# Top-k attention into a mixture of experts: the mask of every third later tile is added by GpSimd

## The chip, the cores and the metric

One core of one Trainium2 chip. The time is that of one execution on the device in microseconds (us); smaller is better. Engine names in the profile: PE is TensorE's matmuls, PEld its weight loads, DVE is VectorE, ACT ScalarE, POOL GpSimd, SP the queue that issues most transfers.

## The reference

Attention over 8 batches of 8 heads, 576 positions, 64 values per head, in which each row keeps its 32 largest scores; then a mixture of 8 experts in which each of the 4608 rows goes to one expert.

```python
scores = scale * np.matmul(q, k.transpose(0, 1, 3, 2))
kth = np.partition(scores, -top_k, axis=-1)[..., -top_k:-top_k + 1]
scores = np.where(scores >= kth, scores, -1000000000.0)
scores = scores - np.max(scores, axis=-1, keepdims=True)
attn = np.exp(scores)
attn = attn / (np.sum(attn, axis=-1, keepdims=True) + 1e-09)
attn_out = np.matmul(attn, v)
...
h = np.maximum(x[mask] @ w1[e], 0.0)
out[mask] = gate_w[mask, None] * (h @ w2[e])
```

## The kernel before

The attention is cut into 288 tiles of 128 rows by 576 scores (9 tiles for each pair of heads, 36 for a batch). One written-out loop of 310 iterations is a software pipeline over them: iteration i computes the scores of tile i+2 on TensorE (`qk`, L336), copies them to SBUF on ScalarE (`sevac`, L342, ten buffers), takes the maxima of seven pieces of tile i on VectorE (`subs`, L349), merges those of tile i-1 to its 24 largest (`chain`, L360 to L362), and lets GpSimd note a bound for them (`below`, L374). Three iterations later ScalarE marks which scores lie below the bound (`sign`, L381), GpSimd multiplies mark and scores (`pool_y`, L387), and VectorE finds the next eight (`find`, L391). Every third iteration `pick` (L398 to L400) sets the 32nd largest, `kth`, for three tiles at once.

The probabilities of tile u = i-7 come at the end of VectorE's share of iteration i. There are two ways. In the first, ScalarE has taken the exponential of all scores an iteration earlier (`expo`, L405), and VectorE compares with `kth`, multiplies and sums in one instruction (`keep`, L411). GpSimd then runs a one-element instruction on the result (`gate`, L434) ahead of its next product L387. In the second, VectorE writes 0 or a large negative number as bfloat16 (`hide`, L418), GpSimd adds it to the scores at the start of its share of iteration u+8 (`hidden`, L424), and ScalarE takes the exponential of the sum and its row sums (`masked`, L430). Which way a tile goes is said by `early(u)`. In the kernel before it is true for two of three tiles up to the 48th, whose masks lie in `hT`, a buffer that the experts need later.

After that TensorE transposes the probabilities (`trans`, L445), ScalarE copies them (`evac`, L453), and `av` multiplies with the values (L473). When a batch is through, its rows are scaled, routed and sent to their expert's place in DRAM: five indirect transfers (`send`, L564), issued by GpSimd, one to an iteration for the second batch on; they stand among VectorE's small steps, ahead of `gate` and `pool_y` in GpSimd's order and behind `hidden`. From then on the loop also carries pieces of the experts' matmuls (L727, L739), as many to an iteration as a written-out budget of TensorE time allows; their output transfers (L754) stand at the end of GpSimd's iteration. Behind the loop, from some 1062 us on, the rest of the experts follows in three-term products.

Each engine runs its own instructions in the order of the program. On GpSimd an iteration's order is: `hidden`, sends and other small steps, `gate`, `pool_y`, `below`, `small` (L368), `fill` (L314), output transfers. On ScalarE: `sign`, copies of the experts' results, `expo`, `sevac`, `evac`, `masked`, splits of the next heads.

`zr` is a constant tile of zeros, which pads the experts' lists in DRAM; its last pad is issued in iteration 26.

Of the kernel before, what the change touches and what calls it, by code (L numbers as in the profile page):

```python
# [11 lines left out]
BF = mybir.dt.bfloat16  # L12
# [51 lines left out]
EARLY = 48  # L64
# [7 lines left out]
def kernel(  # L72
# [14 lines left out]
    B, H, S, D = q.shape  # L87
# [104 lines left out]
    hT = const.tile([128, FC, SLOT], FT, name="hT")  # L192
# [16 lines left out]
    zr = const.tile([128, XW], FT, name="zr")  # L209
# [203 lines left out]
    def hide(i):  # L413

        t = T[i]
        x = 2 * (i % 2)
        t["hb"] = hT[:, x:x + 2, :].rearrange("p f t -> p (f t)").bitcast(BF)[:, :S]
        V.tensor_scalar(t["hb"], t["S"], kth[:, i:i + 1], -HUGE, op0=OP.is_lt, op1=OP.mult)  # L418

    def hidden(i):  # L420
# [34 lines left out]
    def av(p, j, x):  # L455

        vm, vt = LD[p]["v"]
        w = 256 if j < 8 else 64
        st = {}

        def part(c0, c1):
            if c0 == 0:
                st["po"] = psX.tile([128, 256], FT, name="X")
            po = st["po"]
            for c in range(c0, c1):
                for h in range(2):
                    l = vm[:, h, c, :] if c < 4 else vt[:, h if j < 8 else 2 * h, :]
                    if j < 8:
                        r = PT[:, j // 2 - 1:j // 2 + 1, c + 5 * h if c < 4 else 4, :]
                    else:  # L470
                        r = PT[:, 1, 4 + c, h * 64:h * 64 + 64]
                    o = po[h * 64:h * 64 + 64, :w]
                    PE.matmul(o.rearrange("p (a b) -> p a b", a=2) if j < 8 else o, l, r, start=(c == 0), stop=(c == 4))  # L473
            if c1 == 5:
                o = (j // 4) * 256
                xev.append(lambda: A.activation(x[:, o:o + w], po[:, :w], AF.Copy))
        cut = {3: AV3, 7: AV7, 8: (0, 5)}[j]
        return [((b - a) * COST["av" if j < 8 else "av8"], lambda a=a, b=b: part(a, b)) for a, b in zip(cut, cut[1:])]
# [398 lines left out]
        qk(x, 0, x, qbd[0])  # L877
        sevac(x)
    ok = lambda x: 0 <= x < NT
    early = lambda u: u < EARLY and u % 3 != 2  # L880
    dn_of = lambda u: den[(u // 36) % 2][:, (u // 9) % HP, u % 9:u % 9 + 1]
    PREP = dict(zip(PJ, "tkq"))
    spare_pe = 0.0
# [3 lines left out]
    for i in range(LAST):  # L887
# [8 lines left out]
        p, j = divmod(i, 9)  # L896
        u = i - TL
# [11 lines left out]
        u = i - (KL + 1)  # L909
# [6 lines left out]
        u = i - LE  # L916
# [6 lines left out]
        u = i - TL  # L923
        if ok(u):
            evac(u)
        u = i - LR - 1
# [46 lines left out]
        u = i - (TL + 1)  # L973
        if avs:
            c, f = avs.popleft()
            f()
            cost += c
        if ok(u) and u % 9 in (3, 7, 8):
            f = av(u // 9, u % 9, xTs(u // 36)[(u // 9) % HP])
# [9 lines left out]
        while seen[0] and spare_pe > 0:  # L989
# [4 lines left out]
            c, f, new = moe[0]  # L994
# [25 lines left out]
        for x in range(RN if rush else 0):  # L1020
            f = rush.popleft() if rush else PAUSE
# [6 lines left out]
        for x in range(SN - len(small_)):  # L1028
            f = side.popleft() if side and not rush else PAUSE
# [6 lines left out]
        if ok(i - LR):  # L1036
            u = i - LR
            c_.append(lambda u=u: hide(u) if early(u) else keep(u, dn_of(u)))
# [284 lines left out]
```

## Time and profile before

| what | value |
|---|---|
| median of 3 runs | 1294.74 us (1290.1 to 1295.56) |
| profiled execution | 1286.85 us, its span 1285.1 us |
| PE, PEld busy | 1183.2 us (92%), 934.1 us (73%) |
| DVE busy | 1157.5 us (90%) |
| ACT busy | 996.6 us (78%) |
| POOL busy | 665.8 us (52%) |
| granted TensorE clock, mean | 0.984 |

The share of an engine is a mean over stages: the loop over the tiles fills some 20 to 1062 us, the experts' rest the last 220 us. What a change in the loop is worth is read from the loop alone. A busy engine can still be one that waits: TensorE's ends are modelled, and each instruction's end lies beside the start of the next one. So starts are compared with starts.

### The profile page before, as it was taken

How to read it: one execution, taken by the hardware profiler on the slowest of the kernel's cores; microseconds unless marked ns; L12 is line 12 of the kernel's file. 1: busy time of each engine (PE TensorE's matmuls, PEld its weight loads, DVE VectorE, ACT ScalarE, POOL GpSimd, SP SyncE). 2: the span in 40 equal slices, each digit the busy share in tenths (PEclk: the TensorE clock that was granted, in tenths of full speed). 3: DMA queues.
4: the chain of work that ended last, by engine and by line, in shares of the span. 5: the costliest groups of instructions: out<-in, count | busy, mean ns of one | idle time of the engine just before them, and what ended most of it. 6: DMA issues, size and time to landing. Idle time of an engine off the chain costs nothing. (4 is left out here: it accounts for less than half of the span.)

```text
span 1285.1 us, 29038 instructions
## 1 busy us (share of the span) xinstructions
PE 1183.2 (92%) x8117; PEld 934.1 (73%) x8117; DVE 1157.5 (90%) x5948; ACT 996.6 (78%) x2029; POOL 665.8 (52%) x1249
## 2 busy tenths in 40 slices
PE   5789887999988999999999999999999999999996
PEld 4667676767766778686777868777777766789885
DVE  4999999999999999999999999999999992767752
ACT  3799988888888988888898889888988773446542
POOL 2688866555474557554755575556655562110110
PEclk8899999999999999999999999999999999999998
DMA  6565336765347745755665665656766433657550
GB/s 125 125 183 142 89 85 183 198 156 149 85 128 189 216 124 154 199 158 127 194 169 159 168 187 147 171 143 171 170 154 168 132 122 115 234 186 266 204 171 15
DMA packets 206755, 201.05 MB, mean 156 GB/s; under 512 B 106221, under 2 KB 153325, under 8 KB 206576
## 3 DMA queue, kind: packets, MB, share of 16 engines
q1 hardware_dynamic: 198896, 178.59, 52.6%
q0 software_dynamic: 6256, 19.69, 4.2%
q8 instruction: 69, 1.13, 0.4%
q10 hardware_dynamic: 1424, 0.74, 0.2%
q14 instruction: 110, 0.90, 0.2%
HBM read 118.63 MB, written 24.23 MB: 111 GB/s over the span
## 5 line engine op out<-in xcount | busy, mean ns | idle before, releaser
L349 DVE MAX8 cand<-Ssb 128x8 f32<-128x82 f32 (+1 forms) x2016 | 429.4, 230 | 17.9 <-ACT Ssb L342 17.7
L387 POOL TENSOR_TENSOR y<-Ssb,K 128x576 f32<-128x576 f32 x288 | 367.8, 1277 | 1.9 <-ACT K L381 1.6
L336 PE MATMUL S<-ks,qs 128*128 128x288 f32 x1024 | 230.1, 347 | 43.1 <-ACT Ssb L342 24.5
L342 ACT ACTIVATE Ssb<-S 128x576 f32<-128x576 f32 x288 | 188.7, 655 | 91.4 <-PE S L336 61.7
L381 ACT ACTIVATE K<-Ssb,n 128x576 bf16<-128x576 f32 x288 | 227.5, 790 | 25.3 <-POOL y L387 25.1
L336 PEld LDWEIGHTS S<-ks,qs 128*128 128x128 f32 x1024 | 157.4, 192 | 97.0 <-issue 40.5
L391 DVE MAX8 mg<-y 128x8 f32<-128x576 f32 x288 | 214.4, 745 | 2.7 <-POOL y L387 2.7
L405 ACT ACTIVATE ex<-Ssb,sm 128x576 f32<-128x576 f32 x256 | 200.3, 782 | 0.0
L453 ACT ACTIVATE PT<-T 128x640 f32<-128x640 f32 (+1 forms) x288 | 191.1, 663 | 9.5 <-PE T L445 9.5
L727 PE MATMUL E<-xgT,w1b 128*128 128x256 f32 x768 | 187.6, 387 | 6.8 <-ACT hT L731 3.1
L411 DVE SCALAR_TENSOR_TENSOR P<-Ssb,kth,ex 128x576 f32<-128x576 f32 x224 | 188.6, 842 | 0.3
L739 PE MATMUL E<-w2b,hT 128*128 128x512 f32 x384 | 179.6, 596 | 3.0 <-ACT ot L749 1.7
L445 PE MATMUL T<-idf,P 128*128 128x128 f32 x1152 | 171.9, 277 | 9.5 <-ACT P L430 8.9
L727 PEld LDWEIGHTS E<-xgT,w1b 128*128 128x128 f32 x768 | 139.8, 192 | 31.6 <-ACT hT L731 6.4
L434 POOL TENSOR_SCALAR spare<-P 1x1 f32<-1x1 f32 x224 | 43.6, 195 | 201.7 <-DVE mg L360 186.8
L445 PEld LDWEIGHTS T<-idf,P 128*128 128x128 f32 x1152 | 136.0, 141 | 16.7 <-ACT P L430 13.3
L473 PE MATMUL X<-PT,vm 128*64 128x256 f32 (+1 forms) x1536 | 145.6, 332 | 2.4 <-DVE cand L349 1.1
L374 POOL TENSOR_SCALAR n<-mg 128x1 f32<-128x1 f32 x288 | 72.8, 253 | 133.6 <-DVE mg L362 127.0
L473 PEld LDWEIGHTS X<-PT,vm 128*64 128x64 f32 x1536 | 89.2, 137 | 47.8 <-issue 10.1
L739 PEld LDWEIGHTS E<-w2b,hT 128*128 128x128 f32 x384 | 67.2, 190 | 60.6 <-issue 53.2
L1166 POOL DMA_INDIRECT out_dram<-ot,tk x14 | 14.0, 1003 | 132.3 <-ACT ot L1165 132.3
L862 PE MATMUL E<-idf,onesb 128*128 128x256 bf16 x436 | 63.1, 285 | 0.0
(212 smaller groups left out, 2295.8 us busy)
## 6 DMA issues: line engine op xcount, KB each, us to landing
w1b<-in_moe_w_dram SPq DMA_DIRECT2D x76, 512.0 KB, 5.0
w2b<-in_moe_w_dram SPq DMA_DIRECT2D x76, 512.0 KB, 4.9
qs<-st SPq DMA_DIRECT2D x126, 144.0 KB, 3.5
ks<-st SPq DMA_DIRECT2D x63, 288.0 KB, 3.8
ks<-st SPq DMA_DIRECT2D x62, 256.0 KB, 5.2
xg<-xs SPq DMA_DIRECT2D x19, 516.0 KB, 3.9
km<-in_k_dram SPq DMA_DIRECT2D x64, 128.0 KB, 3.5
vm<-in_v_dram SPq DMA_DIRECT2D x32, 256.0 KB, 3.2
```

The source lines that it names most:

```text
L336: PE.matmul(ps[:, hf, u - a:v - a], l, d["ks"][:, x, h, u + o:v + o], start=(n == 0), stop=(n == len(terms) - 1), skip_group_check=(j == 8))
L342: A.activation(sb.rearrange("p (a b) -> p a b", a=2), T[i]["ps"][:, :, :288], AF.Copy, scale=0.125)
L349: return [lambda s=s: V.max(c[:, s * 8:s * 8 + 8], T[i]["S"][:, bnd[s]:bnd[s + 1]]) for s in range(NSUB)]
L381: A.activation(t["K"], t["S"], AF.Sign, scale=2.0 ** -24 - 1.0, bias=t["n"][:, 1, i % 3:i % 3 + 1], accum_out=t["n"][:, 0, i % 3:i % 3 + 1])
L387: G.tensor_tensor(t["y"], t["S"], t["K"], op=OP.mult)
L391: V.max(t["mg"][:, i % 3, 24:32], t["y"])
L405: A.activation(t["ex"], t["S"], AF.Exp, bias=t["s"][:, i % 3:i % 3 + 1])
L445: PE.transpose(T[i]["pt"][:, x, :], (Pm if c == 4 else Pb[c % 2])[:, h * 512 + x * 128:h * 512 + x * 128 + 128], idf)
L453: A.activation(o, T[i]["pt"][:, :n], AF.Copy)
L473: PE.matmul(o.rearrange("p (a b) -> p a b", a=2) if j < 8 else o, l, r, start=(c == 0), stop=(c == 4))
L727: PE.matmul(ps[:, f % 2], w1b[:, c, f * 128:(f + 1) * 128], xgT[:, c, :], start=(c == 0), stop=(c == KC - 1))
L739: PE.matmul(o["py"], hT[:, f, t * 128:(t + 1) * 128], w2b[:, f, :], start=(f == 0), stop=(f == FC - 1))
```

## The change

From tile 48 on, every tile whose number divides by three goes the second way: `hide`, `hidden` and `masked` take the place of `expo`, `keep` and `gate` for it. These are 80 tiles. Their mask lies in `zr` in place of `hT`. The two other tiles of three stay as they are, and so do the first 48.

```diff
-        t["hb"] = hT[:, x:x + 2, :].rearrange("p f t -> p (f t)").bitcast(BF)[:, :S]
+        t["hb"] = (hT[:, x:x + 2, :].rearrange("p f t -> p (f t)") if i < EARLY else zr).bitcast(BF)[:, :S]
         V.tensor_scalar(t["hb"], t["S"], kth[:, i:i + 1], -HUGE, op0=OP.is_lt, op1=OP.mult)
...
-    early = lambda u: u < EARLY and u % 3 != 2
+    early = lambda u: u % 3 != 2 if u < EARLY else u % 3 == 0
```

## Rows read from the trace of the kernel before

**Rows 1.** The page's second part: busy tenths of TensorE and VectorE in 40 equal slices of the span (32 us each).

```profile
PE   5789887999988999999999999999999999999996
DVE  4999999999999999999999999999999992767752
```

**Rows 2.** Busy time of each engine by window: early tiles, and the stretch that the change touches. Columns: length, PE, PEld, DVE, ACT, POOL (instructions), granted clock, DMA share, GB/s.

```profile
48.00:198.00 150.00, 129.59 (x1090) 103.50 (x1091) 150.00 (x825) 136.06 (x308) 119.34 (x167) 0.99 0.48 119
198.00:1062.00 864.00, 821.90 (x5601) 632.80 (x5600) 851.93 (x4621) 739.36 (x1519) 501.43 (x976) 0.99 0.61 161
```

**Rows 3.** VectorE's costliest groups from 198 to 1062 us: count | busy us, mean ns | idle us before them, and who ended it.

```profile
L349 DVE MAX8 cand<-Ssb 128x8 f32<-128x82 f32 x1161 | 260.7, 231 | 0.0
L411 DVE SCALAR_TENSOR_TENSOR P<-Ssb,kth,ex 128x576 f32<-128x576 f32 x213 | 178.4, 838 | 0.3
L391 DVE MAX8 mg<-y 128x8 f32<-128x576 f32 x237 | 176.8, 746 | 2.7 <-POOL y L387 2.7
```

**Rows 4.** Who waited for whom from 198 to 1062 us: us in total, times, longest.

```profile
ACT Ssb L342 <- PE S L336: 39.7, 46, 2.3
ACT K L381 <- POOL y L387: 25.1, 47, 1.7
...
PE S L336 <- ACT Ssb L342: 19.3, 25, 2.3
```

**Rows 5.** VectorE in order of time, a tile that divides by three and the next one: start us, us, what.

```profile
943.31 0.82 DVE L411 SCALAR_TENSOR_TENSOR P<-Ssb,kth,ex 128x576 f32<-128x576 f32 x1
944.06 0.08 DVE L411 DVE_READ_ACCUMULATOR P<-Ssb,kth,ex 128x1 f32 x1
...
946.48 0.80 DVE L411 SCALAR_TENSOR_TENSOR P<-Ssb,kth,ex 128x576 f32<-128x576 f32 x1
```

**Rows 6.** VectorE in order of time among the early tiles: two instructions L418, what follows each, and the L411 behind the second.

```profile
116.54 0.49 DVE L418 TENSOR_SCALAR hT<-Ssb,kth 128x576 bf16<-128x576 f32 x1
116.95 0.20 DVE L360 MAX8 mg<-cand 128x8 f32<-128x56 f32 x1
...
119.37 0.58 DVE L418 TENSOR_SCALAR hT<-Ssb,kth 128x576 bf16<-128x576 f32 x1
119.87 0.20 DVE L360 MAX8 mg<-cand 128x8 f32<-128x56 f32 x1
...
122.29 0.96 DVE L411 SCALAR_TENSOR_TENSOR Pm<-Ssb,kth,ex 128x576 f32<-128x576 f32 x1
123.18 0.08 DVE L411 DVE_READ_ACCUMULATOR Pm<-Ssb,kth,ex 128x1 f32 x1
```

**Rows 7.** GpSimd in order of time beside the second half of rows 6.

```profile
118.36 1.28 POOL L387 TENSOR_TENSOR y<-Ssb,K 128x576 f32<-128x576 f32 x1
...
120.10 1.28 POOL L424 TENSOR_TENSOR ex<-Ssb,hT 128x576 f32<-128x576 f32 x1
121.34 1.29 POOL L387 TENSOR_TENSOR y<-Ssb,K 128x576 f32<-128x576 f32 x1
```

**Rows 8.** GpSimd in order of time beside rows 5 (in brackets: idle before it, and who ended that).

```profile
944.30 0.18 POOL L434 TENSOR_SCALAR spare<-P 1x1 f32<-1x1 f32 x1 [1.43 <-DVE mg L360]
944.45 1.27 POOL L387 TENSOR_TENSOR y<-Ssb,K 128x576 f32<-128x576 f32 x1
```

**Rows 9.** VectorE in order of time: end of a step L411 and start of the next L411, for the first (tile 60) and the last (tile 279) of the 32 tiles that divide by three, have a gap of at most 2.50 us and no send in their iteration.

```profile
244.03 0.08 DVE L411 DVE_READ_ACCUMULATOR P<-Ssb,kth,ex 128x1 f32 x1
...
246.44 0.80 DVE L411 SCALAR_TENSOR_TENSOR P<-Ssb,kth,ex 128x576 f32<-128x576 f32 x1
...
1042.33 0.08 DVE L411 DVE_READ_ACCUMULATOR P<-Ssb,kth,ex 128x1 f32 x1
...
1044.74 0.80 DVE L411 SCALAR_TENSOR_TENSOR P<-Ssb,kth,ex 128x576 f32<-128x576 f32 x1
```

**Rows 10.** GpSimd's groups from 198 to 1062 us: the sends.

```profile
L564 POOL DMA_INDIRECT xs<-x,dest x35 | 37.5, 1073 | 7.9 <-issue 4.2 <-DVE cand L349 2.5 <-DVE mg L360 0.8
```

**Rows 11.** VectorE in order of time within one burst of sends: two instructions L411 and the end of their steps.

```profile
757.72 1.93 DVE L411 SCALAR_TENSOR_TENSOR P<-Ssb,kth,ex 128x576 f32<-128x576 f32 x1
759.58 0.08 DVE L411 DVE_READ_ACCUMULATOR P<-Ssb,kth,ex 128x1 f32 x1
...
761.99 1.38 DVE L411 SCALAR_TENSOR_TENSOR P<-Ssb,kth,ex 128x576 f32<-128x576 f32 x1
763.31 0.08 DVE L411 DVE_READ_ACCUMULATOR P<-Ssb,kth,ex 128x1 f32 x1
```

**Rows 12.** GpSimd in order of time beside rows 11.

```profile
757.76 1.27 POOL L387 TENSOR_TENSOR y<-Ssb,K 128x576 f32<-128x576 f32 x1
...
760.12 1.03 POOL L564 DMA_INDIRECT xs<-x,dest  x1 [0.16 <-issue]
...
761.48 1.27 POOL L387 TENSOR_TENSOR y<-Ssb,K 128x576 f32<-128x576 f32 x1
```

**Rows 13.** Line 411 over the whole span: shortest/median/longest ns, first and last start us.

```profile
L411 DVE SCALAR_TENSOR_TENSOR P<-Ssb,kth,ex x224: 787/802/1930, 47.6 to 1059.2; 128x576 f32<-128x576 f32 x112
```

**Rows 14.** Groups of the whole span: the exponential of the first way, the add and the exponential of the second.

```profile
L405 ACT ACTIVATE ex<-Ssb,sm 128x576 f32<-128x576 f32 x256 | 200.3, 782 | 0.0
...
L424 POOL TENSOR_TENSOR ex<-Ssb,hT 128x576 f32<-128x576 f32 x32 | 41.1, 1284 | 17.6 <-DVE hT L418 10.9 <-DVE mg L360 5.5
...
L430 ACT ACTIVATE P<-ex,sm 128x576 f32<-128x576 f32 x32 | 25.2, 788 | 0.0
```

## The prediction

> **What bounds the kernel now.** I read the busy digits first, then the stretch that the change touches, then who waits there, then single instructions. The change starts with tile 48; that tile's probability step stands near 198 us and the last one ends near 1062 us. In that stretch VectorE is busy for 851.9 of 864 us; TensorE shows 821.9, ScalarE 739.4, GpSimd 501.4 [rows 1, 2]. Two engines near full, so the question is which one waits for the other. VectorE's sub-maxima L349, the first thing it does with new scores, had 0.0 us of idle time ahead of 1161 of them, and the full-row maximum L391 2.7 us in 237 tiles [rows 3]: VectorE's inputs are ready before it wants them. TensorE does wait, for the copy that frees its scores buffer (19.3 us), ScalarE waits for scores (39.7 us) and for GpSimd's product (25.1 us) [rows 4]. So VectorE sets the pace, and what is taken off it in this stretch should come off the time, as long as the others' slack holds. TensorE's granted clock is 0.99 and is no part of this.
>
> A busy time overstates VectorE's cost, since one instruction's end overlaps the next one's start. I count steps instead: from an instruction's start to the start of the next on the engine.
>
> **The change part by part.** From tile 48 on, 80 tiles (48, 51, ... 285) go the hidden way.
>
> *VectorE, removed and added.* L411 is a step of 0.75 us (943.31 to 944.06) [rows 5]. L418 in its place was 0.41 us (116.54 to 116.95) where no GpSimd product ran beside it, and 0.50 where 0.27 us of one did [rows 6, 7]. In the new order the third-tile's L418 comes late in an iteration, when GpSimd's product is long done (the product ends at 945.72, the next L411 starts at 946.48 [rows 5, 8]), so I take 0.42. Saved: 80 x 0.33 = 26 us, all of it on the pacing engine.
>
> *What the next tile pays for it.* Today GpSimd runs gate and product L387 behind L411: both are over 1.66 us after L411's step ends (944.06 to 945.72) [rows 5, 8]. Behind L418 it runs the add L424 and then L387, over 2.76 us after (119.87 to 122.63) [rows 6, 7]. The next tile's L411 can start 2.42 us after (122.29; the same 2.42 from 944.06 to 946.48) [rows 5, 6]. So the tail of L387 runs into it by 0.34 us, and L411 took 0.89 us there in place of 0.75 [rows 6]: 0.14 given back. Where VectorE has other small work in that iteration, L411 starts later and escapes. I took the gap from the end of L411's step to the next L411 for the 78 tiles 48 to 279: 38 are at most 2.50 us (the first of the plain ones and the last are in [rows 9]), 13 lie between 2.50 and 2.75, 27 are longer. Six of the 38 belong to the bursts below. 32 x 0.14 + 13 x 0.07 = 5.4 us given back.
>
> The row says that 0.34 us of overlap cost 0.14. The Trainium skill, "SBUF — State Buffer", section "Who interferes with whom", says that a VectorE instruction with two SBUF inputs contends with a GpSimd instruction that reads SBUF, and that the pair of ports is an exclusive lock for a whole instruction; by that the cost would be the 0.34 whole, 32 x 0.34 + 13 x 0.15 = 13 us in place of 5.4.
>
> *The bursts of sends.* Each batch from the second on sends its rows in five GpSimd transfers L564, one to an iteration, of 1.07 us each; the window has 35, of which 30 are of this kind [rows 10]. They are queued ahead of gate today, so they run beside L411 and cost it nothing. The add is queued ahead of them: L424, then L564, then L387, which then begins about 2.8 us after L418 and sits on the next L411 from its start. What that costs the trace shows in one burst: an L411 that began with L387 took 1.86 us (757.72 to 759.58), one with 0.76 us of L387 left took 1.32 [rows 11, 12]: 1.1 and 0.57 over the plain step. And it persists: with a send in each iteration GpSimd doesn't catch up, so the next L411 is hit too. Five iterations in a row hold one or two hidden tiles. Lower end: nothing, if the add fits. Upper end: one at 1.1 and four at 0.57, 3.4 us x 6 = 20 us. A part is paid already: L411 means 838 against a median of 802, 36 ns x 213 = 7.7 us [rows 3, 13]. I take one at 1.1 and two at 0.57, 2.24 x 6 = 13.5, less 6 that is paid now: 7.5 us given back.
>
> *ScalarE.* L405 (782 ns) goes, L430 (788 ns) and an accumulator read come [rows 14]; at the 0.1 to 0.2 us that a read can add to the queue, 8 to 16 us over 80 tiles. It is hidden by ScalarE's 125 us of idle time in the stretch [rows 2]; if that cover were gone it would cost these 8 to 16.
>
> *New waits.* L424 waits for L418; behind it in GpSimd's queue stand the sends, L387, the bound L374 and the output transfers. L387 later by 1.1 us has L391 waiting for it, which had 2.7 us of waits in 237 tiles, so cover is there save in bursts. The score copy L342 reuses the buffer that L424 now reads last, so it may wait 1.3 us longer in one tile of three, and behind it stand the PT copy, L430 and the next sign L381. TensorE's next scores wait for that copy, yet VectorE sat idle for scores 0.0 us [rows 3]; I cost it at nothing, and at up to 3 us if a queue runs dry near the start. GpSimd's load grows by 80 x (1.28 - 0.18) = 88 us to 589 of 864. The Trainium skill ("GPSIMD Engine Reference", section "4.1 Engine selection") sends a two-input elementwise op to VectorE and calls GpSimd about two times slower; 1.28 us against 0.84 here agrees in direction [rows 3, 14], and would matter only if GpSimd became the pace. Using zr as the mask costs nothing: its last pad transfer is issued 29 iterations before its first use.
>
> Sum: -26 + 5.4 + 7.5 = -13 us. The profiled execution took 1286.85 us, 1.75 over its span, and would become 1274. The median of the three runs is 1294.74, 7.9 above it; I carry the difference over: 1281.5.
>
> **The rivals.**
> Full gain: the overlaps stay out, as in the 27 long gaps, and bursts get no worse: -26, 1268.7. Against it: the early tiles show the overlap in the same order of instructions [rows 6, 7].
> Whole blocking: each overlap costs its full length, as nearly seen with the long ones (1.1 of 1.31, 0.57 of 0.76 [rows 11, 12]), though not with the short one. Then 13 in place of 5.4, and 1.3 and 0.76 in the bursts (2.8 x 6 - 6 = 11): -26 + 13 + 11 = -2, about 1293.
> Absorbed: TensorE at 95% busy [rows 2] or ScalarE takes over the pace and VectorE starts to wait for scores; then some 5 us remain, 1290. Against it: they wait for VectorE's buffers now.
> Slower: GpSimd falls out of step outside the bursts too, so that after every hidden tile an L411 begins with 0.76 us or more of L387 still to run. Each then pays 0.57 against 0.33 saved: 80 x 0.24 = +19, 1314. It decides when the loss per hidden tile passes 0.33 us, between the overlaps of 0.34 and 0.76. For it: GpSimd needs close to 4 us in an iteration that holds an add (1.28), a send (1.07), L387 (1.28) and the small ones. Against it: the two tiles of three without an add leave it idle again.
> No effect: L418 on zr isn't the quick step of 0.41 but as long as L411; then no gain, 1295 to 1300. The input and output types are the early tiles', which speaks against it.
>
> **How the numbers follow.** Forecast 0.57, full gain 0.10, whole blocking 0.06, absorbed 0.14, slower 0.10, no effect 0.03. The forecast's own range is 1270 to 1290, by the burst bounds (0 to 12 given back beyond what is paid) and the short overlaps. Half a per cent is 6.5 us, about what a measurement of this kernel can tell from no change. Of the forecast 0.52 lies below 1288.3, with full gain 0.10 and a quarter of whole blocking and absorbed 0.05: faster 0.67. Slower: 0.10 and a little of no effect, 0.11. The rest, 0.22, is the same. Low 1268 takes in the full gain; high 1294 leaves out the slower case and part of no effect.
>
> **What would show it.** In the new trace: L418 at 0.41 to 0.50 us a step, 112 of them; L411 160 times late, those after a hidden tile at 0.89 where the gap is 2.42 and 0.75 elsewhere; long ones (over 1.1 us) only near the sends, about 18 in all; L349 still with no idle time. TensorE's waits for the score copy should stay or shrink. The forecast is wrong if L349 or L391 show many microseconds of idle time (absorbed), or if L411's mean outside the bursts rises above 1.1 us (slower).

## The result and the profile after

The changed kernel takes 1303.64 us (median of 7 runs), the kernel before 1291.53 us on the same chip (7 runs): 1.0091 times as long, with a 95% interval of 1.0074 to 1.0107. It is 12.1 us slower where I forecast 13 us faster. The profiled execution is 1299.5 us (span 1297.7) against 1286.85.

The page of the new kernel, busy digits, first TensorE, then VectorE:

```profile
PE   5788887999988999999999999999999999999986
DVE  3999999999999999999899999999999993757752
```

Nothing is to be seen there beside [rows 1]: a VectorE that stands inside an instruction counts as busy. The window of the change, with the columns of [rows 2]:

```profile
198.00:1062.00 864.00, 819.14 (x5554) 625.63 (x5553) 844.79 (x4522) 738.40 (x1584) 594.09 (x967) 0.99 0.60 160
```

GpSimd went from 501 to 594 us, as worked out (589). VectorE is 7 us less busy and has done 99 instructions fewer in the same window. Most of these aren't missing work: each hidden tile saves the read of L411's sum, 84 of those reads are gone from the window, and the kernel is later in its work at 1062 us. Its groups there, with the columns of [rows 3]:

```profile
L349 DVE MAX8 cand<-Ssb 128x8 f32<-128x82 f32 x1163 | 260.0, 229 | 0.0
...
L391 DVE MAX8 mg<-y 128x8 f32<-128x576 f32 x234 | 174.3, 745 | 7.0 <-POOL y L387 7.0
L411 DVE SCALAR_TENSOR_TENSOR P<-Ssb,kth,ex 128x576 f32<-128x576 f32 x130 | 123.5, 950 | 0.0
L418 DVE TENSOR_SCALAR zr<-Ssb,kth 128x576 bf16<-128x576 f32 x78 | 40.4, 518 | 0.0
...
L500 DVE TENSOR_SCALAR rd<-den 128x36 f32<-128x36 f32 x6 | 3.6, 607 | 0.0
...
L587 DVE TENSOR_TENSOR r_pr<-r_pb,ohb 128x40 f32<-128x40 f32 x6 | 3.0, 498 | 0.0
```

L411 rose from a mean of 838 ns to 950, and two groups that I had not looked at belong to VectorE's small steps, some 340 of them in this stretch, which route a batch's rows to the experts. L500 writes 36 numbers for each partition and L587 40, and they take half a microsecond. Line 587 over the whole span, shortest, median, longest ns, first in the kernel before:

```profile
L587 DVE TENSOR_TENSOR r_pr<-r_pb,ohb x8: 174/182/665, 192.8 to 1082.2; 128x40 f32<-128x40 f32 x8
```

and after:

```profile
L587 DVE TENSOR_TENSOR r_pr<-r_pb,ohb x8: 171/349/973, 194.6 to 1094.3; 128x40 f32<-128x40 f32 x8
```

The longest one, VectorE of the changed kernel in order of time (start us, us, what):

```profile
341.43 0.50 DVE L418 TENSOR_SCALAR zr<-Ssb,kth 128x576 bf16<-128x576 f32 x1
341.85 0.20 DVE L360 MAX8 mg<-cand 128x8 f32<-128x56 f32 x1
...
343.81 0.97 DVE L587 TENSOR_TENSOR r_pr<-r_pb,ohb 128x40 f32<-128x40 f32 x1
344.71 0.24 DVE L349 MAX8 cand<-Ssb 128x8 f32<-128x83 f32 x1
```

and GpSimd beside it:

```profile
342.01 1.28 POOL L424 TENSOR_TENSOR ex<-Ssb,zr 128x576 f32<-128x576 f32 x1 [1.39 <-DVE zr L418]
...
343.43 1.29 POOL L387 TENSOR_TENSOR y<-Ssb,K 128x576 f32<-128x576 f32 x1
```

The add pushes the product back to 343.43, L587 begins 0.38 us into it, and VectorE's next instruction starts at 344.71, when the product ends (343.43 + 1.29 = 344.72). An instruction of 0.18 us (the median before) took 0.97. The waits of the stretch, in the manner of [rows 4]:

```profile
ACT Ssb L342 <- PE S L336: 46.4, 59, 2.9
ACT Ssb L342 <- POOL ex L424: 17.2, 17, 2.3
...
DVE mg L391 <- POOL y L387: 7.0, 9, 1.5
...
DVE lt L535 <- PE X L527: 3.9, 4, 1.5
...
DVE x L507 <- PE X L506: 3.0, 4, 1.6
```

The second line is new: the score copy waits for the add that still reads its buffer. The last three are VectorE's own waits, for the late product and for two results of TensorE.

To put all this into one sum I added up VectorE's steps, start to start with idle time apart, from the probability step of tile 48 to that of tile 284 (us; "small" are the 337 small steps, "maxima" L349 and L360 to L362, "pick" L398 to L400; the groups that didn't move, L391, L538 and reads of PSUM, are left out). Each row is one execution, and the executions of the kernel before alone spread from 1287.8 to 1299.6 us, so a difference of two or three us in a stretch says little:

| kernel | stretch | L411 and its reads | L418 | small | maxima | pick | idle |
|---|---|---|---|---|---|---|---|
| before | 857.1 | 179.2 | 0 | 32.6 | 425.3 | 28.4 | 9.9 |
| after | 869.3 | 134.6 | 34.4 | 48.3 | 422.7 | 28.4 | 19.2 |
| after - before | +12.2 | -44.6 | +34.4 | +15.7 | -2.6 | 0 | +9.3 |

The stretch holds the whole loss: 12.2 of 12.65 us between the profiled executions. Hiding and keeping together are 10.2 us cheaper. The small steps took 15.7 us and the waits 9.3.

What the small steps stood for can be read one by one. Of the 42 that took over 0.05 us longer than their line's median in the kernel before, 40 ended within 0.1 us of the end of a GpSimd two-input instruction: 37 of a product L387, 3 of an add. The steps beside such an instruction hold all of the 15.7 us. Not all of them read two tiles: 6.0 us are in steps that read one, `tensor_scalar` (L500 2.7, L645 1.2) and a copy (L667 1.2) above all.

L411 keeps a rule of the same kind. Alone its step is 0.73 us. The 57 L411 of the changed kernel that began more than 0.2 us before the end of a product or add that was already running ended 0.54 to 0.56 us after that end, whatever the overlap. So each lost its overlap less 0.18 us.

### The profile page after: what moved, and what is told of

Read it like the earlier page. It is cut to its first block, busy times and chain, and to the rows that moved or that the text cites. A ratio compares the mean times of both kernels' runs of the same rounds, so it can differ in the third digit from the quotient of the medians.

```text
span 1297.7 us, 28859 instructions
## 1 busy us (share of the span) xinstructions
PE 1189.3 (92%) x8117; PEld 933.3 (72%) x8117; DVE 1161.7 (90%) x5868; ACT 1003.1 (77%) x2109; POOL 767.1 (59%) x1249
## 5 line engine op out<-in xcount | busy, mean ns | idle before, releaser
L349 DVE MAX8 cand<-Ssb 128x8 f32<-128x82 f32 (+1 forms) x2016 | 428.2, 229 | 19.0 <-ACT Ssb L342 18.9
L387 POOL TENSOR_TENSOR y<-Ssb,K 128x576 f32<-128x576 f32 x288 | 367.9, 1277 | 6.2 <-ACT K L381 5.7
L381 ACT ACTIVATE K<-Ssb,n 128x576 bf16<-128x576 f32 x288 | 228.8, 795 | 15.4 <-POOL y L387 15.2
L391 DVE MAX8 mg<-y 128x8 f32<-128x576 f32 x288 | 214.2, 744 | 7.1 <-POOL y L387 7.0
L445 PE MATMUL T<-idf,P 128*128 128x128 f32 x1152 | 173.4, 278 | 17.9 <-ACT P L430 17.2
L374 POOL TENSOR_SCALAR n<-mg 128x1 f32<-128x1 f32 x288 | 85.7, 298 | 108.9 <-DVE mg L362 96.2
L424 POOL TENSOR_TENSOR ex<-Ssb,zr 128x576 f32<-128x576 f32 x80 | 103.0, 1287 | 63.3 <-DVE zr L418 60.8
L405 ACT ACTIVATE ex<-Ssb,sm 128x576 f32<-128x576 f32 x176 | 138.6, 787 | 0.0
L411 DVE SCALAR_TENSOR_TENSOR P<-Ssb,kth,ex 128x576 f32<-128x576 f32 x144 | 136.8, 950 | 0.0
L430 ACT ACTIVATE P<-ex,sm 128x576 f32<-128x576 f32 x112 | 88.7, 792 | 0.6 <-POOL ex L424 0.6
```

The source lines that it names most:

```text
L349: return [lambda s=s: V.max(c[:, s * 8:s * 8 + 8], T[i]["S"][:, bnd[s]:bnd[s + 1]]) for s in range(NSUB)]
L381: A.activation(t["K"], t["S"], AF.Sign, scale=2.0 ** -24 - 1.0, bias=t["n"][:, 1, i % 3:i % 3 + 1], accum_out=t["n"][:, 0, i % 3:i % 3 + 1])
L387: G.tensor_tensor(t["y"], t["S"], t["K"], op=OP.mult)
L391: V.max(t["mg"][:, i % 3, 24:32], t["y"])
L405: A.activation(t["ex"], t["S"], AF.Exp, bias=t["s"][:, i % 3:i % 3 + 1])
L445: PE.transpose(T[i]["pt"][:, x, :], (Pm if c == 4 else Pb[c % 2])[:, h * 512 + x * 128:h * 512 + x * 128 + 128], idf)
```

## The experiments

Theory after the result: while GpSimd runs a two-input instruction, VectorE's two-input instructions, the small ones too, and some one-input ones stand until it ends; the add makes more of that time and pushes the product onto the small steps. Rivals: the saving was never there, since TensorE caps the loop; the score buffer that the add holds; the place of the add in GpSimd's queue. Sums "of the loop" are by the table's method in the profiled execution; times are medians beside the kernel before on the same chip. The code shown is each edit's main lines; `...` marks what is left out.

### The saving without the add

`e1_no_add` leaves the add out: the exponential reads the bare scores at the add's place.

```diff
+        if i >= EARLY:
+            t["z"] = t["S"]
+            return
...
```

> The changed kernel without GpSimd's add: for the 80 tiles VectorE still writes the mask, but ScalarE takes the exponential of the bare scores (the mask isn't applied for these tiles), and GpSimd's one-element gate stands where it stood before the change. Ports theory (GpSimd's add makes its two-input instructions run beside VectorE instructions that share its ports): all that was given back is gone and the whole saving of 79 x 0.32 = 25 us stays, 1266 us. Waits theory (the path mask, add, exponential, and the product that comes later behind the add): the waits are gone as well, also 1266. Other-engines theory (VectorE's saving never came through because TensorE or ScalarE take over the pace): 1285 or more.

Measured: 1339.39 us, 1.0363 (1.0324 to 1.0402). The edit spoiled itself: the loop is 878.4 us with 46.5 idle. I put that down to the late exponential, which holds the score buffer until ScalarE comes to it; and the mask that isn't applied changes which rows go where, so that the work behind the loop differs. It decides nothing.

`e1b_no_add` takes that exponential at `expo`'s place, so that the buffer is free as early as before. Only the loop can be compared.

```diff
+        if ok(u) and early(u) and u >= EARLY:
+            T[u]["z"] = T[u]["S"]
+            masked(u, dn_of(u))
...
```

> The changed kernel without GpSimd's add, mended: ScalarE takes the exponential of the bare scores for the 80 tiles at the place of the old exponential (the mask isn't applied, so rows are routed to other experts and the work behind the loop is another); VectorE writes the mask, GpSimd's gate stands where it stood. So the loop alone is compared, from tile 48's probability step to tile 284's: 857.1 us before, 869.3 in the changed kernel. Ports and waits theories: the saving of 25 us comes through, 832. Other-engines theory: 852 or more.

Measured: loop 848.7 us, 8.4 less than before (whole time 1302.91, one run, with the other tail); the exponential's place was worth 29.7 us of e1's loop. L411 119.9 and L418 34.3, so 25.0 us less than 179.2 came off VectorE's work, small steps 33.5, but idle 27.3. Two of VectorE's groups from 198 to 1040 us:

```profile
L411 DVE SCALAR_TENSOR_TENSOR P<-Ssb,kth,ex 128x576 f32<-128x576 f32 x130 | 109.2, 840 | 0.9 <-ACT ex L405 0.9
L418 DVE TENSOR_SCALAR zr<-Ssb,kth 128x576 bf16<-128x576 f32 x78 | 40.3, 516 | 0.0
```

and its waits:

```profile
DVE x L508 <- PE X L507: 9.2, 8, 2.1
DVE lt L536 <- PE X L528: 5.9, 4, 1.8
DVE mg L391 <- POOL y L387: 5.1, 9, 0.9
```

(L508 is L507 of the other kernels.) The saving is real, and two thirds of it is waited away, most of that on two of TensorE's results (15.1 us, where the kernel before waited 2.3). To see whether it is TensorE's load that does so, `e12_before_less_pe` and `e13_no_add_less_pe` lower the budget of TensorE time that the experts' pieces get, in the kernel before and in e1b.

```diff
-STEP = 3.39
+STEP = 3.1
```

> The kernel before with the budget for TensorE cut from 3.39 to 3.1 us an iteration, so that fewer pieces of the experts are computed in the loop and more behind it. Control for the next run; the loop alone is compared (tile 48's probability step to tile 284's, 857.1 us before). TensorE-cap theory and ports theory alike: VectorE sets the pace, so the loop shortens only by the expert-choosing steps that leave it, 845 to 857.

> The run without the add (loop 848.7 us, 8.4 shorter than before; the mask isn't applied, so rows are routed otherwise and only the loop is compared) with the same cut of TensorE's budget. TensorE-cap theory (of the 25 us that VectorE saves, 15 went into waits for TensorE's batch rows): with less TensorE work the loop is 20 to 25 us shorter than its control's. Own-delay theory (the moved exponential or the missing add delays something else): again about 8 shorter.

Measured: loops 854.8 and 834.8 us, a gain of 20.0 where it was 8.4; idle 9.9 and 15.2. (Whole times 1308.95 and 1310.1, one run each: the pieces that the loop lost come behind it.) So at this load a third of VectorE's saving comes through, and with less load on TensorE four fifths (20.0 of 24.2), as far as one execution of each shows. That limits a gain; it doesn't make a loss.

### The price of an add without the saving

Four kernels keep the first way for all late tiles and add idle work on GpSimd for the same tiles. `e2_add_only` adds zeros to the scores in place at the start of GpSimd's iteration, where `hidden` would stand, with that tile's `gate` ahead of it; `e10_add_elsewhere` adds on the constant tile `zr` there (128x516), which no one waits for.

```diff
...
+        if extra:
+            gate(i - 1 - LR)
+            G.tensor_tensor(t["S"], t["S"], zr.bitcast(BF)[:, :S], op=OP.add)     # e2
+            G.tensor_tensor(zr, zr, zr, op=OP.add)                                # e10
...
```

> The kernel before, with GpSimd's add alone: for the same 80 tiles, at the same place in GpSimd's order, gate and then an add of a tile of zeros to the scores in place (after their last use); the probabilities are made the old way. Ports theory: no saving, and all that the change gives back: L411 15, small VectorE steps 16, the late product 7 us, together 1291.5 + 38 = 1329. Waits theory: only the late product and the score buffer that comes free later, since nobody waits for the sum: 1298. Other-engines theory: 1291.

> The run with the add alone (1331.6 us), but the add works on a constant tile (516 elements a partition) that nobody else reads in the loop, at the same place ahead of the product. So the score buffer comes free as early as before the change. Ports theory: VectorE's L411 and small steps still meet product and add, 1291.5 + 35 = 1327. Buffer theory (a large part of the 40 us is the score copy that waits for its buffer, and TensorE behind it): L411 and small steps pay the same, yet the time falls well below, to 1300 to 1315.

Measured: e2 1331.62 us, 1.0301 (1.0268 to 1.0334); e10 1317.13, 1.0211 (1.0182 to 1.0239), loops 899.8 and 885.3. Two groups of e10 from 200 to 1080 us:

```profile
L411 DVE SCALAR_TENSOR_TENSOR P<-Ssb,kth,ex 128x576 f32<-128x576 f32 x208 | 187.1, 899 | 0.0
...
L587 DVE TENSOR_TENSOR r_pr<-r_pb,ohb 128x40 f32<-128x40 f32 x6 | 2.9, 477 | 0.0
```

and GpSimd's add:

```profile
L898 POOL TENSOR_TENSOR zr<-zr 128x516 f32<-128x516 f32 x78 | 80.8, 1036 | 0.2 <-issue 0.2
```

e10's loop is 28.2 us longer with 0.7 us more idle time: 14.0 in L411 (193.2), 14.1 in the small steps (46.7). No buffer is held and nothing more is waited for; it is the standing alone, 0.35 us for each add of 1.04 us, and it is as much as the whole saving (25.0). Of the small steps that were lengthened, 37 end with the product that the add pushed back and 3 with the add itself. e2 is 14.5 us above e10: L411 and the small steps pay 11.2 of this, and idle time 2.8. Its add is longer (1.27 us) and holds a buffer; which of the two makes the 11.2 isn't separated. There the copy waits:

```profile
ACT Ssb L342 <- POOL Ssb L899: 61.4, 52, 2.8
```

`e7_add_behind_product` puts e2's add behind `pool_y`; `e8_memset_behind_product` writes the same scores there three times, which reads nothing; `e9_memset_elsewhere` writes `zr` three times.

```diff
...
+        if ok(u) and u >= EARLY and u % 3 == 0:
+            G.tensor_tensor(t["S"], t["S"], zr.bitcast(BF)[:, :S], op=OP.add)     # e7
+            for _ in range(3): G.memset(t["S"], 0.0)                              # e8
+            for _ in range(3): G.memset(zr, 0.0)                                  # e9
```

> The kernel before with the add alone (zeros added to the scores in place, after their last use), behind the product in place of ahead of it. The product is as early as before the change. Ports theory: the add now stands where the product stood, and reads two inputs as it does, so L411 and the small steps pay about the same: 1291.5 + 31 = 1322. Late-product theory (the 38 us of the add alone are waits for a product that comes late): 1292 to 1296.

> As the run with the add behind the product, but GpSimd writes zeros over the same dead scores three times, which reads nothing. Ports theory: nothing stands in VectorE's way, 1291 to 1295. Busy-GpSimd theory (whatever GpSimd does there delays its bound, its sends and the score buffer): as with the add, to the extent of the time it takes, 1305 to 1322.

> The run with three memsets behind the product (1317.6 us), but on the same constant tile in place of the dead scores: GpSimd is as busy, reads nothing and holds no score buffer. Buffer theory: the waits of the score copy go, 1292 to 1297. Busy-GpSimd theory (late bound, sends and product): 1310 or more. Ports theory: 1292, as for the run before it.

Measured: 1330.81 us, 1.0307 (1.0268 to 1.0346); 1317.59, 1.0193 (1.0154 to 1.0233); 1302.87, 1.0088 (1.0066 to 1.011). Loops 896.0, 886.0, 871.8. e9's groups from 200 to 1080 us on GpSimd:

```profile
L1059 POOL MEMSET zr<- 128x516 f32 x240 | 126.3, 526 | 9.2
```

and on VectorE:

```profile
L411 DVE SCALAR_TENSOR_TENSOR P<-Ssb,kth,ex 128x576 f32<-128x576 f32 x212 | 177.7, 838 | 0.5 <-ACT ex L405 0.4
...
L587 DVE TENSOR_TENSOR r_pr<-r_pb,ohb 128x40 f32<-128x40 f32 x6 | 1.1, 184 | 0.0
```

GpSimd is occupied for 126 us by writes, half as long again as by e10's adds, and L411 is at 838 ns, as in [rows 3], and L587 at 184; L411 sums to 179.5 (e9) and 180.2 (e8) against 179.2 before, with e7's add to 192.0. It is an instruction that reads (two tiles here; one that reads a single tile wasn't tried) that L411 stands for, not a busy GpSimd. Both e8 and e9 are well above what the ports theory expected (1291 to 1295 and 1292). What e9 costs is idle time (+9.4; L391's wait for the late product rose by 7.4 to 10.1) and 5.8 in the small steps. Its trace puts 5.0 of the 5.8 on steps that stood for the product, which the writes had made late: 13 of those ended within 0.1 us of a product's end. e8 is 14.2 us of loop above e9, 11.0 of it idle time; it holds the score buffer (and its writes are 575 ns in place of 526). Its copy waited 78.4 us for the memset, and e9's had no such wait:

```profile
ACT Ssb L342 <- POOL Ssb L1060: 78.4, 46, 4.0
```

### Another place, another buffer

`e3_add_behind_sends` moves `hidden` and `masked` behind the sends, ahead of `pool_y`.

```diff
+        if ok(u) and early(u) and u >= EARLY:
+            hidden(u)
+            masked(u, dn_of(u))
...
```

> The changed kernel with add and second exponential of the late tiles moved from the start of an iteration to gate's place, behind the sends and the small steps in GpSimd's order and behind the copies in ScalarE's. Ports theory: the sends no longer stand between add and product, so the long L411 near the sends go back to what they were, 8 us of the 12 come back, 1296; the small VectorE steps still meet the product. Waits theory: the sum comes later for ScalarE and TensorE, 1304 or more.

Measured: 1317.31 us, 1.0195 (1.0157 to 1.0234), 24.6 us slower than before, so worse than the change and 21 us above what I expected. The small steps stay at 48.9 and L411 at 135.7; idle time is 25.6, of it 11.3 for TensorE's L506. This other place in the queue spares the standing nothing.

`e11_one_more_buffer` gives the scores an eleventh buffer (and takes one from the products); `e14_before_11buf` does so to the kernel before.

```diff
-YB = 3
+YB = 2
...
-        T[i]["S"] = sb = wk.tile([128, S], FT, name="Ssb", bufs=LR + 1 + QL - QO)
+        T[i]["S"] = sb = wk.tile([128, S], FT, name="Ssb", bufs=LR + 2 + QL - QO)
```

> The changed kernel with eleven score buffers in place of ten, paid for by two product buffers in place of three. Buffer theory: the 17 us in which the score copy waited for the add go, and with them the waits of VectorE for TensorE and for the product, 1303.6 - 8 = 1296. Ports theory: nothing changes, 1303.

> The kernel before with eleven score buffers and two product buffers. Control for the changed kernel with the same (1298.3, 5.3 less than without). Buffer theory (the buffer matters because the add holds it): no change here, 1290 to 1294. If the buffer helps any kernel: 1286 to 1289.

Measured: 1298.31 us, 1.0056 (1.0038 to 1.0075); 1290.57, 0.9995 (0.9978 to 1.0011). The buffer is worth some 5 us (1.0091 to 1.0056 is 4.5, 12.1 to 5.7 us above before is 6.4) only where the add holds one, and the wait of the copy for the add is gone from e11's list. The small steps stay at 48.5. How the buffer brings its gain the sums don't settle: between the two profiled executions, only 1.2 us apart (1298.32 and 1299.5), L411 is 4.1 us lower and idle time 1.9 higher.

### Which tiles

A tile u is called quiet here if iteration u+8, in which its add runs, holds none of VectorE's small steps, no send and no list of rows. Of the 80 tiles 34 are quiet, 46 busy. `e4_clean_tiles` hides the quiet ones alone, `e5_busy_tiles` the others.

```diff
-    early = lambda u: u % 3 != 2 if u < EARLY else u % 3 == 0
+    LATE = (60, 63, 66, 72, 75, 78, 81, 90, 102, 108, 114, 126, 138, 141, 150, 153, 162, 177, 180, 186, 189, 198, 213, 216, 225, 246, 249, 252, 258, 261, 267, 270, 279, 285)
+    early = lambda u: u % 3 != 2 if u < EARLY else u in LATE
```

> Of the 80 tiles only the 34 whose add falls into an iteration without small VectorE steps, sends or transfers of rows go the hidden way. Ports theory: they save 34 x 0.32 and give back 34 x 0.14 on the next L411, 1291.5 - 6 = 1285. Waits theory: each hidden tile costs the same, 34 of 80 of the loss of 12, so 1296.5.

> The other 46 of the 80 tiles go the hidden way: those whose add falls into an iteration with small VectorE steps (routing, choosing an expert), sends or rows' tokens. Ports theory: all of the loss is here and none of the gain of the 34 others, 1303.6 + 6 = 1310. Waits theory: 46 of 80 of the loss, 1298.5.

Measured: e4 1288.7 us, 0.9973 (0.9954 to 0.9993); e5 1306.9, 1.0103 (1.0076 to 1.0131). e4, from 198 to 1062 us:

```profile
L500 DVE TENSOR_SCALAR rd<-den 128x36 f32<-128x36 f32 x6 | 1.0, 167 | 0.0
```

and e5:

```profile
L500 DVE TENSOR_SCALAR rd<-den 128x36 f32<-128x36 f32 x6 | 3.6, 608 | 0.0
```

By the sums e4 has its small steps at 32.8 (before: 32.6), L411 and L418 together 5.2 below before, idle 4.1 above: loop -2.4. e5 has L411 and L418 8.7 below, small steps 15.8 above, idle 13.2 above: loop +19.3. The busy tiles hold all of the loss, and all of the small steps' 15.7. The two don't add up (-2.4 + 19.3 = 16.9, the change is 12.2), so they aren't independent.

If quiet tiles gain, more of them might gain more: `e6_all_clean` hides 109 quiet tiles from 48 on, whatever their number. `e15_clean_11buf` and `e16_all_clean_11buf` give e4 and e6 the eleventh buffer.

> A version meant to be faster: of all tiles from the 49th on, those 109 go the hidden way whose add falls into an iteration without small VectorE steps, sends or row tokens, whatever their number. Ports theory: 109 x 0.32 saved, about 0.14 to 0.2 given back each, 1291.5 - 15 = 1277. Buffer theory: the score buffer is freed late three times as often as in the run with 34 tiles, so the gain is eaten, 1290. Other-engines theory (TensorE close behind VectorE): not below 1283.

> A version meant to be faster: the 34 tiles whose add falls into a quiet iteration (1288.7) with eleven score buffers and two product buffers. Buffer theory: 34 of 80 of the 5.3 us come back as well, 1286. TensorE-cap theory: no more than 1287 to 1289, since VectorE's saving already meets TensorE.

> The version with 109 hidden tiles, whatever their number (1301.9), with eleven score buffers and two product buffers. Buffer theory: the adds of neighbouring tiles hold the score buffers and delay TensorE, so the eleventh brings it back to 1290 or below. TensorE-cap theory: VectorE's steps are shorter than before by 20 us or more, and its waits for TensorE and ScalarE are longer by as much or more; about 1295 to 1302, with or without the buffer.

Measured: e6 1301.9 us, 1.0076 (1.0058 to 1.0095), 25 us above what I expected; e15 1286.91, 0.9954 (0.9938 to 0.9971); e16 1296.73, 1.0032 (1.0013 to 1.0051). The profiled execution of e6 took 2364.83 us, so rows are read from one more run of its kernel, `e17_all_clean_again` (1300.25 us).

> The version with 109 hidden tiles once more, for its profile, since the earlier profiled execution was a disturbed one. Buffer theory: the score copy waits for the add for 30 us or more. TensorE-cap theory: VectorE waits for TensorE's products, 15 us or more against 2 before.

VectorE's groups of e17 from 198 to 1060 us:

```profile
L418 DVE TENSOR_SCALAR zr<-Ssb,kth 128x576 bf16<-128x576 f32 x107 | 62.1, 581 | 0.6 <-POOL ex L424 0.3 <-issue 0.3
...
L398 DVE TENSOR_TENSOR eq<-i9s,n 128x27 f32<-128x27 f32 x78 | 39.5, 506 | 0.0
L399 DVE TENSOR_TENSOR jk<-eq,mg 128x27 f32<-128x27 f32 x78 | 16.9, 217 | 0.1
```

and of before:

```profile
L398 DVE TENSOR_TENSOR eq<-i9s,n 128x27 f32<-128x27 f32 x79 | 17.6, 223 | 0.0
L399 DVE TENSOR_TENSOR jk<-eq,mg 128x27 f32<-128x27 f32 x79 | 16.8, 213 | 0.1
```

The small steps are spared (32.9), and the next two-input step in line is hit: L398 of `pick`, 223 to 506 ns, as the tiles are now of all three kinds and `pick` comes every third iteration (38 of its L398 were lengthened, and 37 ended within 0.04 us of the end of a product or add); `pick` is 22.6 us up, idle time 13.3. L411 and L418 are 23.8 down: 22.6 + 13.3 - 23.8 = +12.1 of 12.5. Why one more buffer helps this kernel by 5 us isn't settled by these rows: e16's idle time is 3.3 lower. e15 has the lowest time of the study, 5.4 us below before; its interval overlaps e4's, so that it beats e4 isn't shown. Its profiled execution was its slowest of 13, so its rows aren't set against e4's.

## Why the prediction was wrong

*VectorE sets the pace, and what is taken off it comes off the time.* True as far as it went: L349 still has 0.0 us of idle time. But of 25 us only 8.4 come through without the add (e1b), 20.0 where TensorE has less to do (e13 against e12). The rival in which TensorE absorbs the gain was right in kind. By itself it couldn't turn the sign.

*Saved 26.* Right: 25.0 in e1b. L418 took steps of 0.435 us on average, 0.42 was assumed.

*The next L411 and the bursts, 5.4 + 7.5.* Right in size: 134.6 against 119.9 without the add is 14.7 given back. The forecast sum was near, its parts less so: 25 late L411 last over 1.1 us, 13 of them right behind hidden tiles, where about 18 in all were forecast. The 0.14 of 0.34 us in [rows 6, 7] is no milder price than the 1.1 of 1.31 and the 0.57 of 0.76 in [rows 11, 12]: all three L411 end their step 0.55 or 0.56 us after the product, and all lose the overlap less some 0.2 us. So L411 stands for the whole of the product even there, and the rival of whole blocking, which would have given back 24, was right in kind and too high.

*The step that failed.* "Where VectorE has other small work in that iteration, L411 starts later and escapes." L411 does; the small work doesn't. It was treated as a spacer that keeps L411 out of the product, and it stands there itself: 15.7 us, for which the sum has no term. A blocked 40-wide instruction loses as much as a blocked 576-wide one: 40 of the 42 that were lengthened ended with GpSimd's instruction. e10 shows it with no new wait (14.1), e4 and e5 show where (0.2 in quiet tiles, 15.8 in busy ones). The rule that I weighed there bears on this: the Trainium skill, "SBUF — State Buffer", section "Who interferes with whom", has a two-SBUF-input VectorE instruction contend with a GpSimd instruction that reads SBUF, not with one that only writes, and calls the shared ports an exclusive lock. L587 stood until the product's end to 0.01 us, and the memsets of e8 and e9 left L411 alone (180.2, 179.5). I priced that rule for L411 alone, the longest instruction in its reach, and not for the rest. Nor did I look at one-input steps, which took 6.0 of the 15.7 us.

*ScalarE 0.* Right: its busy time in the window is 738.4 after 739.4, and L411 waits 0.0 us for exponentials.

*New waits: "nothing", "up to 3 us".* Too small: 9.3. 4.3 of it is L391 waiting for the late product (7.0 after 2.7), which I had covered "save in bursts"; 4.6 are waits for TensorE (L507 0.7 to 3.0, L535 1.6 to 3.9). The wait of the score copy that I had named is there, 17.2 us, and it does cost something: the eleventh buffer removes it and gives some 5 us, though VectorE's own idle time doesn't fall with it.

By terms: -25.0 + 14.7 + 15.7 + 9.3 - 2.6 + 0.1 = +12.2. Against the forecast's -13.1 the small steps are 15.7 off, the waits 9.3, the maxima -2.6, L411 1.8, the saving and rests 1.1.

*The rivals.* "Slower" had the sign and not the mechanism: it wanted 0.57 us from each L411 behind a hidden tile, and the mean step of those L411 rose by 0.18 (0.748 to 0.925), well under the 0.33 saved.

What stays open: how the maxima came to be 2.6 us shorter, by which way the held buffer costs its 5 us, and what the 22.6 us of `pick` and the 13.3 of idle time in e17 owe to each other.

## What to carry to other kernels

Before work goes to GpSimd, list every VectorE instruction that will lie beside it and reads two tiles, and the one-input `tensor_scalar` and copies too, small ones first in number, and price each at the time left of GpSimd's instruction, not at its own length; here, for an add that no one waited for, that alone was as much as the saving (28.2 against 25.0 us). Then ask which buffer the slower engine will hold, and how much of the saving the second busiest engine lets through. Moving only where none of the small steps is a neighbour, here 34 of 80 tiles with a buffer more, kept a small gain (0.9954).

## What the hardware showed that I had not expected

VectorE's L500, which adds a constant to one tile, 36 wide, stands as well: 167 ns in e4, 608 in e5. Which one-input steps do and which don't isn't settled here.

An L411 can stand for a product that begins after it. VectorE of the changed kernel:

```profile
901.44 2.61 DVE L411 SCALAR_TENSOR_TENSOR P<-Ssb,kth,ex 128x576 f32<-128x576 f32 x1
903.98 0.07 DVE L411 DVE_READ_ACCUMULATOR P<-Ssb,kth,ex 128x1 f32 x1
```

and GpSimd:

```profile
901.08 0.99 POOL L564 DMA_INDIRECT xs<-x,dest  x1 [0.17 <-issue]
902.13 1.29 POOL L387 TENSOR_TENSOR y<-Ssb,K 128x576 f32<-128x576 f32 x1
```

It began 0.69 us ahead of the product, almost the length that it needs (0.75), and its step ended at 903.98, 0.56 us after the product did (903.42). It isn't the only one: five L411 of the changed kernel began 0.29 to 0.79 us ahead of a product with an indirect transfer beside their start, and all ended 0.55 or 0.56 us after the product. Three with such a transfer beside their start and no product behind took 0.72 or 0.73 us. One that began 0.24 us ahead of an add with no transfer beside it wasn't held, and the add took 1.72 us in place of 1.28:

```profile
1072.72 0.81 DVE L411 SCALAR_TENSOR_TENSOR P<-Ssb,kth,ex 128x576 f32<-128x576 f32 x1
1073.46 0.08 DVE L411 DVE_READ_ACCUMULATOR P<-Ssb,kth,ex 128x1 f32 x1
```

```profile
1072.96 1.72 POOL L424 TENSOR_TENSOR ex<-Ssb,zr 128x576 f32<-128x576 f32 x1 [1.56 <-ACT xT L476]
```

So it took both, the transfer and the product right behind it; by which way, no run tells.
